# Sparse attention and a multiplicative FFN on one core: strided rows block-major, v cast by its load, probabilities transposed by DMA

## The chip, the cores and the metric

The kernel runs on one core of one Trainium2 chip. The metric is the device time of one execution in microseconds. Three executions of the kernel before took 291.08, 290.63 and 291.65 us; the median is 291.08 us. A separate execution was profiled, and all rows below come from it.

## The reference, cut to what matters

```python
batch, n_heads, seq, head_dim = (8, 8, 576, 64)         # q, k, v in fp32
scores = scale * np.matmul(q, k.transpose(0, 1, 3, 2))
rel = pos[:, None] - pos[None, :]
mask_local = (rel >= 0) & (rel < 32)                    # heads 0 to 3
mask_strided = (rel >= 0) & (pos[None, :] % 32 == pos[:, None] % 32)   # heads 4 to 7
...                                                     # softmax over the masked scores, times v
x = attn_out.transpose(0, 2, 1, 3).reshape(4608, 512)
a = x @ w1                                              # w1, w2: 512 x 1024
b = x @ w2
h = a * b @ w3                                          # w3: 1024 x 1024
out = h @ w_out                                         # w_out: 1024 x 512
```

A strided head attends only among the 18 positions that share a residue modulo 32, so its scores fall into 32 blocks of 18 x 18. A local head attends to a band of 32.

## The kernel before

**Pairs.** The 64 heads are worked in 32 pairs of two heads; pair `i` belongs to batch `i // 4`, and in each batch the first two pairs are local and the last two strided. A pair passes through these steps, each a function of the pair's number:

- `load_qk`: POOL issues loads of q and k that cast fp32 to fp16 on the way, two DMAs for a local pair (line 87), four for a strided one (line 97), into a tile with four buffers.
- `load_v`: SP issues loads of v in fp32, three for a local pair (lines 111, 113), six for a strided pair (line 123). `emit_cast_v` then casts v to fp16 on POOL (line 265 local, line 269 strided), and for a local pair `shift_v` lets SP copy the cast tile to a second one moved by 32 rows (lines 277 and 278, tile `vhL`).
- `emit_T`: TensorE (PE in the profile) transposes q and k (line 289); ACT and DVE copy the results out of PSUM.
- `emit_S`: score matmuls (line 321 local, 328 strided), mask added by DVE. `emit_max`, `emit_sub`, `emit_exp`: maximum and subtraction on DVE, exponential on ACT into `prL` or `prS`.
- `emit_norm`: row sum and reciprocal on DVE (lines 369, 371), product on POOL (line 372). It is called norm(i) below.
- `emit_P`: TensorE transposes the probabilities, five 128x128 blocks for a local pair and six for a strided one (line 382, tile `pp` in PSUM); ACT copies them to SBUF as `pT` (line 385). Called P(i) below.
- `emit_V`: matmuls of v and `pT` (line 402 local, 417 strided), results copied to `xT`, the FFN's input. Called V(i).

Three residues are packed side by side on the partitions in a strided pair: 3 x 18 = 54 rows per head. Row p holds residue group `p // 18` and block `p % 18`.

**FFN.** First w3 and w_out are folded into one 1024 x 512 matrix (`fold_t`, `fold_m`, lines 218 to 229). Then chunks of 512 tokens go through `emit_a` (line 236), `emit_b` (line 246, product on DVE at line 249) and `emit_out` (line 254, copied by ACT, stored by SP at line 258).

**Order.** The order of the work is written out by hand; each engine executes its own instructions in program order. Pairs 0 to 4 are written call by call, then a loop covers n = 5 to 8, then a main loop n = 9 to 33. An iteration n of the main loop issues `load_qk(n+4)`, `load_v(n+3)`, `shift_v(n)`, S(n), V(n-2), T(n+1), max, sub, exp of n, P(n-1), norm(n) and `emit_cast_v(n+1)`. Between them `feed(us, batches)` puts in FFN pieces by a credit of us per call, 5.2 us per iteration in the main loop, as far as the batches needed are there. After the loop, the remaining FFN pieces follow without attention work between them.

**Queues.** SP issues the stores of the output, the loads of v and the shifts; POOL issues the casting loads and also computes. Within each of the two queues the program gives DMAs eight completion semaphores in turn, and a DMA waits for the one eight places before it in its queue to have landed. Whatever stands behind a waiting DMA on POOL waits too, norm among it. The PSUM pool `psA`, with two buffers, holds the transposed q and k and, in turn, `pp`.

Of the kernel before, what the change touches and what calls it, by code (L numbers as in the profile page):

```python
# [8 lines left out]
FP32 = mybir.dt.float32  # L9
# [18 lines left out]
def kernel(  # L28
# [40 lines left out]

    NB = 2  # L70
    staged, cast, qks, prs, pts = {}, {}, {}, {}, {}

    def where(i):
        b, hp = divmod(i, 4)
        return b, hp, hp < 2, (2 * b + hp % 2) % NB

    def load_qk(i):

        b, hp, local, par = where(i)
        h0 = 2 * hp  # L80
        t = ld.tile([P, 2, ST * D], FP16, tag="s16", bufs=4, name="s16")
        if i + 1 == 4 * B:
            for p0 in (0, HALF):
                nc.vector.memset(t[p0 + 32:p0 + HALF, :, (ST - 1) * D:ST * D], 0.0)
        for src, p0 in ((q, 0), (k, HALF)):
            if local:
                nc.gpsimd.dma_start(t[p0:p0 + HALF, :, 0:LB * D],
                                    src[b, h0:h0 + 2].rearrange("h (p j) d -> p h (j d)", j=LB))
            elif i + 1 == 4 * B:
                for r in range(3):  # L90
                    n = ST if r < 2 else ST - 1
                    nc.gpsimd.dma_start(t[p0 + NA * r:p0 + NA * r + NA, :, 0:n * D],
                                        _ap(src[b, h0], 11 * r * D,
                                            [[NR * D, NA], [S * D, 2], [1, n * D]]))
            else:
                for h in range(2):
                    nc.gpsimd.dma_start(t[p0:p0 + SW, h, :],  # L97
                                        _ap(src[b, h0 + h], 0,
                                            [[11 * D, 3], [NR * D, NA], [1, ST * D]]))
        cast[i] = t  # L100

    def load_v(i, gate=False):
# [3 lines left out]
        if local:  # L106
            vt = vsL[par]
            if gate:
                nc.vector.memset(vt[:, 0:LC - 1, 0, 0:1], 0.0)
            for h in range(2):  # L110
                nc.sync.dma_start(vt[:, 0:LC - 1, h, :],
                                  _ap(v[b, h0 + h], 0, [[D, P], [P * D, LC - 1], [1, D]]))
            nc.sync.dma_start(vt[0:HALF, LC - 1],
                              v[b, h0:h0 + 2, P * (LC - 1):S].rearrange("h p d -> p h d"))
        else:
            vt = vsS[par]
            if gate:
                nc.vector.memset(vt[:, :, 0:1], 0.0)
            for r in range(3):
                for half in range(2):  # L120
                    n = 6 if half == 0 else 5 if r < 2 else 4
                    p0 = HALF * half + NA * r
                    nc.sync.dma_start(vt[p0:p0 + NA, :, 0:n * D],
                                      _ap(v[b, h0], (11 * r + 6 * half) * D,
                                          [[NR * D, NA], [S * D, 2], [1, n * D]]))
        staged[i] = vt
# [3 lines left out]
    maskS = consts.tile([P, SW], FP32, name="maskS")  # L130
    sel = consts.tile([3, HALF], FP16, name="sel")
    sel2 = consts.tile([3, 2, HALF], FP16, name="sel2")
# [16 lines left out]
    def make_sel():  # L149
        nc.gpsimd.memset(sel, 1.0)  # L150
        nc.gpsimd.affine_select(out=sel, in_=sel, compare_op=ALU.is_ge, fill=0.0, base=0,
                                pattern=[[1, HALF]], channel_multiplier=-NA)
        nc.gpsimd.affine_select(out=sel, in_=sel, compare_op=ALU.is_ge, fill=0.0, base=NA - 1,
                                pattern=[[-1, HALF]], channel_multiplier=NA)

    def make_maskS():
        for h in range(2):
            nc.vector.tensor_copy(out=sel2[:, h, :], in_=sel)
        mps = psF.tile([P, SW], FP32, tag="f", name="mps")
        nc.tensor.matmul(mps, sel2.rearrange("p h q -> p (h q)"), sel[:, 0:SW], start=True,  # L160
                         stop=True)
# [16 lines left out]
    prS = [wpool.tile([P, 12, HALF], FP16, name=f"prS{i}") for i in range(NB)]  # L178
    vsS = [wpool.tile([P, 2, 6 * D], FP32, name=f"vsS{i}") for i in range(NB)]
    vsL = [wpool.tile([P, LC, 2, D], FP32, name=f"vsL{i}") for i in range(NB)]  # L180
# [80 lines left out]
    def emit_cast_v(i, eng=nc.gpsimd.tensor_copy):  # L261
        b, hp, local, par = where(i)
        vst = staged.pop(i)
        if local:
            eng(out=vhL[par][:, 1], in_=vst)
            pts[i] = [vhL[par]]
        else:
            vh = att.tile(list(vst.shape), FP16, tag="vhS", name="vh")
            eng(out=vh, in_=vst)
            pts[i] = [vh.rearrange("p h (t d) -> p t h d", d=D)]  # L270

# [92 lines left out]
    def emit_norm(i):  # L364
# [8 lines left out]
                                op=ALU.mult)  # L373

    def emit_P(i):

        b, hp, local, par = where(i)
        pr = prs.pop(i)[0]
        n = LC if local else 6
        pp = psA.tile([P, n, P], FP16, tag="tr", name="pp")  # L380
        for s in range(n):
# [6 lines left out]
    def emit_V(i):  # L388
# [20 lines left out]
        else:  # L409
            ops = [psF.tile([P, 6 - half, SW], FP32, tag="f", name="op") for half in range(2)]  # L410
            for s in range(6):
                for half in range(2):
# [3 lines left out]
                    for h in range(2):  # L416
# [4 lines left out]
            nc.scalar.copy(out=_sub(xT[hp], 0, P, x0, [[NR, NA], [11, 3], [1, 6]]),  # L421
                           in_=_sub(ops[0], 0, P, 0, [[1, NA], [NA, 3], [SW, 6]]))
            nc.vector.tensor_copy(out=_sub(xT[hp], 0, P, x0 + 6, [[NR, NA], [11, 2], [1, 5]]),
                                  in_=_sub(ops[1], 0, P, 0, [[1, NA], [NA, 2], [SW, 5]]))
            nc.vector.tensor_copy(out=_sub(xT[hp], 0, P, x0 + 28, [[NR, NA], [1, 4]]),
                                  in_=_sub(ops[1], 0, P, 2 * NA, [[1, NA], [SW, 4]]))

# [3 lines left out]

    NP = 4 * B
    T_A = 0.87
# [31 lines left out]
    with tc.manual_schedule():  # L465
# [54 lines left out]
        emit_cast_v(1)  # L520
        shift_v(1)
        load_qk(5)
        fold_t(3, act)
# [7 lines left out]
        emit_max(3)  # L531
        emit_cast_v(2)
        load_w12(1)
# [8 lines left out]
        emit_norm(3)  # L542
        emit_cast_v(3)
        load_v(4, True)
# [16 lines left out]
        emit_exp(4)  # L561
        load_v(6, True)
        load_v(7)
# [5 lines left out]
        for n in range(5, 9):  # L569
# [8 lines left out]
            if n > 5:  # L578
                emit_V(n - 2)
                load_v(n + 2)  # L580
            emit_sub(n)
# [4 lines left out]
            if n == 8:  # L586
# [3 lines left out]
                shift_v(8)  # L590
                load_v(11)
        for n in range(9, NP + 2):
# [62 lines left out]
```

## Time and profile before

| what | value |
|---|---|
| median of three executions | 291.08 us (290.63 to 291.65) |
| the profiled execution's own time | 291.78 us |
| its span, first to last instruction | 290.1 us |
| mean granted TensorE clock | 0.994 |
| busy: PE, DVE, ACT, POOL | 262.0, 175.8, 157.7, 130.0 us |
| PE transposes of probabilities (line 382), in all 32 pairs | 176 blocks of 128x128 |
| ACT copies of them (line 385) | 32, of 685 ns (local) and 791 ns (strided) |
| POOL casts of strided v (line 269) | 16 of 848 ns |

The table's busy times are unions over the whole span; the parts of the span differ, so they are read together with the windows and chains below. "PE" is the matmul row, "PEld" its weight loads, "SPq" an instruction of SP's queue that only issues. In a chain of waits each line has a start, a length in us and what the time was spent on; in a timeline each line has a start, a length, the engine, the line, the operation, its output and input, and a count, with the idle time before it in brackets.

### The profile page before, as it was taken

What the parts mean: (1) busy time and instruction counts of PE and PEld (TensorE: products, weight loads), DVE (VectorE), ACT (ScalarE), POOL (GpSimd) and SP (SyncE); (2) the same over time, 40 slices, a digit from 0 to 9 for tenths busy, and PEclk for the clock granted to TensorE, in tenths of its full rate; (3) what the DMA queues carried; (4) which work ended last, traced back from release to release, by engine and by line L of the source; (5) the groups of instructions that cost most, each with busy time, mean ns of one, the idle gap of its engine ahead of it and who ended that gap; (6) DMA issues with size and microseconds to landing.
All of it is one profiled execution on the core that took longest, in us unless ns stands there. A gap on an engine that the chain in (4) does not pass through costs nothing.

```text
span 290.1 us, 10150 instructions
## 1 busy us (share of the span) xinstructions
PE 262.0 (90%) x4305; PEld 138.1 (48%) x4305; DVE 175.8 (61%) x342; ACT 157.7 (54%) x282; POOL 130.0 (45%) x186
## 2 busy tenths in 40 slices
PE   1179768987989999999999999999999999999994
PEld 0045434444445555555555555555555554444441
DVE  3716545688658866785788677768857860441210
ACT  3225654544656765676666667756767554333322
POOL 8655737256665644674465456446732210000000
PEclk9999999999979999999999999999999999999999
DMA  7999999946797777765966796778522003000113
GB/s 113 188 211 208 181 214 157 178 94 118 144 190 177 112 157 173 155 101 137 210 102 86 179 190 98 134 170 166 107 96 97 2 2 123 22 2 36 73 52 129
DMA packets 58893, 36.90 MB, mean 127 GB/s; under 512 B 37088, under 2 KB 53216, under 8 KB 58848
## 3 DMA queue, kind: packets, MB, share of 16 engines
q0 software_dynamic: 27584, 14.88, 37.1%
q1 hardware_dynamic: 31264, 21.38, 26.5%
q8 instruction: 33, 0.54, 0.8%
q14 instruction: 12, 0.10, 0.1%
HBM read 39.07 MB, written 9.44 MB: 167 GB/s over the span
## 4 chain that ended last, share of the span: by engine, by line
PE 76%; DMA 8%; POOL 5%; DVE 4%; issue 3%; ACT 2%; SPq 0%; POOLq 0%; DVEq 0%; ACTq 0%
PE ops L254 21%; PE bps L246 20%; PE aps L236 20%; DMA s<-in_k_dram 4%; DMA vhL<-vhL 4%; PE pp L382 3%; PE tpk L289 2%; PE sp L328 2%; PE sp L321 2%; PE op L402 2%; PE op L417 1%; PE tpq L289 1%; PE fps L227 1%; DVE sm L369 1%; DVE tmp L334 1%
## 5 line engine op out<-in xcount | busy, mean ns | idle before, releaser
L249 DVE TENSOR_TENSOR abt<-bps,asb 128x512 f16<-128x512 f32 x72 | 49.6, 688 | 41.0 <-PE bps L246 37.9
L246 PE MATMUL bps<-xT,w2h 128*128 128x512 f16 x288 | 74.1, 380 | 0.0
L236 PE MATMUL aps<-xT,w1h 128*128 128x512 f16 x288 | 74.0, 379 | 0.0
L254 PE MATMUL ops<-wfh,abt 128*128 128x512 f16 x288 | 68.1, 385 | 0.0
L240 ACT COPY asb<-aps 128x512 f32<-128x512 f32 x72 | 42.4, 588 | 35.9 <-PE aps L236 35.8
L257 ACT COPY osb<-ops 128x512 f32<-128x512 f32 x36 | 21.1, 586 | 41.1 <-PE ops L254 37.9
L254 PEld LDWEIGHTS <-abt 128*128 128x128 f16 x288 | 27.4, 99 | 31.5 <-issue 1.7
L372 POOL TENSOR_TENSOR prL<-prL,rc 128x576 f16<-128x576 f16 x16 | 18.3, 1146 | 51.6 <-DVE rc L371 42.6
L246 PEld LDWEIGHTS <-w2h 128*128 128x128 f16 x288 | 26.5, 98 | 30.0
L236 PEld LDWEIGHTS <-w1h 128*128 128x128 f16 x288 | 27.1, 98 | 28.7
L372 POOL TENSOR_TENSOR prS<-prS,rc 128x594 f16<-128x594 f16 x16 | 19.2, 1198 | 41.5 <-DVE rc L371 20.7
L349 DVE TENSOR_TENSOR tmp<-tmp,mx 128x576 f32<-128x576 f32 (+1 forms) x32 | 26.5, 829 | 1.0
L342 DVE TENSOR_REDUCE mx<-tmp 128x9 f32<-128x576 f32 (+1 forms) x32 | 24.1, 753 | 0.2
L385 ACT COPY pT<-pp 128x640 f16<-128x640 f16 (+1 forms) x32 | 23.6, 738 | 0.3 <-PE pp L382 0.3
L334 DVE TENSOR_TENSOR tmp<-sp,maskL 128x320 f32<-128x320 f32 (+1 forms) x32 | 13.2, 453 | 15.9 <-PE sp L321 15.9
L289 PE MATMUL tpq<-id,s 54*64 54x54 f16 (+1 forms) x640 | 17.7, 196 | 5.2 <-DMA s<-in_q_dram 5.1
L97 POOL DMA_DIRECT2D s<-in_k_dram x30 | 18.0, 611 | 6.5 <-DMA w3s<-in_moe_w_dram 2.3
L289 PEld LDWEIGHTS <-s 54*64 54x64 f16 (+1 forms) x1280 | 15.7, 110 | 9.2 <-DMA s<-in_q_dram 6.3
L289 PE MATMUL tpk<-id,s 54*64 54x54 f16 (+1 forms) x640 | 18.4, 198 | 1.8 <-DMA s<-in_k_dram 1.7
L97 POOL DMA_DIRECT2D s<-in_q_dram x30 | 19.1, 643 | 0.4 <-DMA s<-in_q_dram 0.3
L369 DVE TENSOR_REDUCE sm<-prL 128x9 f32<-128x576 f16 x16 | 12.0, 749 | 11.8 <-ACT prL L361 11.8
L361 ACT ACTIVATE prS<-tmp 128x594 f16<-128x594 f32 x16 | 11.2, 699 | 12.1 <-DVE tmp L349 10.2
(75 smaller groups left out, 304.0 us busy)
## 6 DMA issues: line engine op xcount, KB each, us to landing
out_dram<-osb SPq DMA_DIRECT2D x36, 256.0 KB
vsL<-in_v_dram SPq DMA_DIRECT2D x32, 128.0 KB
vsS<-in_v_dram SPq DMA_DIRECT2D x48, 54.0 KB
s<-in_q_dram POOLq DMA_DIRECT2D x16, 144.0 KB, 4.3
s<-in_k_dram POOLq DMA_DIRECT2D x16, 144.0 KB, 5.3
s<-in_q_dram POOLq DMA_DIRECT2D x30, 74.2 KB, 5.7
s<-in_k_dram POOLq DMA_DIRECT2D x30, 74.2 KB, 6.5
w3s<-in_moe_w_dram POOLq DMA_DIRECT2D x4, 512.0 KB, 12.0
```

The lines of the kernel that those rows point to most:

```text
L97: nc.gpsimd.dma_start(t[p0:p0 + SW, h, :], _ap(src[b, h0 + h], 0, [[11 * D, 3], [NR * D, NA], [1, ST * D]]))
L236: nc.tensor.matmul(aps, w1h[:, ci, jc * P:(jc + 1) * P], xT[ci][:, c * NT:(c + 1) * NT], start=(ci == 0), stop=(ci == KC1 - 1))
L240: nc.scalar.copy(out=asb, in_=aps)
L246: nc.tensor.matmul(bps, w2h[:, ci, jc * P:(jc + 1) * P], xT[ci][:, c * NT:(c + 1) * NT], start=(ci == 0), stop=(ci == KC1 - 1))
L249: nc.vector.tensor_mul(abts[c][:, jc, :], bps, abts.pop((c, jc)))
L254: nc.tensor.matmul(ps, abts[c][:, jc, ts * P:(ts + 1) * P], wfh[:, jc, :], start=(jc == 0), stop=(jc == KC2 - 1))
L257: nc.scalar.copy(out=osb, in_=ps)
L289: nc.tensor.transpose(tp[HALF * h:HALF * h + HALF, s, :], s16[p0:p0 + npar, h, s * D:(s + 1) * D], id16[p0:p0 + npar, p0:p0 + npar])
L342: nc.vector.tensor_reduce(out=mx, in_=tmp, axis=AX.X, op=ALU.max)
L349: nc.vector.tensor_tensor(out=tmp, in0=tmp, in1=_sub(mx, 0, P, 0, [[1, nt], [0, w]]), op=ALU.subtract)
L372: nc.gpsimd.tensor_tensor(out=prv, in0=prv, in1=_sub(rc, 0, P, 0, [[1, nt], [0, w]]), op=ALU.mult)
L385: nc.scalar.copy(out=pT, in_=pp)
```

## The change

Three things change.

1. In strided pairs the 54 rows are ordered with the block first: row p now holds block `p // 3` and residue group `p % 3`. The mask's selector, the loads and the copies from PSUM into `xT` follow. For the last pair, whose last row would run past the tensor, the second head is loaded by four smaller DMAs.
2. v of a strided pair is loaded by four DMAs of POOL that cast to fp16 into a tile `vhS` with four buffers, where six fp32 DMAs of SP and a cast on POOL stood. The two cleared fp32 buffers `vsS` go. For the last pair ten DMAs take the place of the four. These loads come later in the written order: `load_v(2)` behind `load_w3(3)`, `load_v(3)` behind `shift_v(1)`, and in the main loop two pairs ahead of use where it was three.
3. From pair 9 on (`XB = 9`) P(i) is a single transposing DMA issued by SP from `prL` or `prS` straight into `pT`, in place of five or six TensorE transposes and one ACT copy. It is issued at the end of iteration i, where P(i) on TensorE stood in the middle of iteration i+1. V(i) stays in iteration i+2.

On POOL a strided pair thus has eight DMA issues where it had four, and no cast. On SP six issues per strided pair go and one transposing DMA per pair comes.

```diff
+    NP, XB = 4 * B, 9
...
+    def strided_rows(i, h, n):
+
+        if i + 1 < 4 * B or h == 0:
+            return [((0, SW), (0, [[NR * D, NA], [11 * D, 3]]), n)]
+        e = NR * D * (NA - 2)
+        return [((0, SW - 6), (0, [[NR * D, NA - 2], [11 * D, 3]]), n),
+                ((SW - 6, SW - 3), (e, [[11 * D, 3]]), n),
+                ((SW - 3, SW - 1), (e + NR * D, [[11 * D, 2]]), n),
+                ((SW - 1, SW), (e + NR * D + 22 * D, [[D, 1]]), n - 1)]
...
                 for h in range(2):
-                    nc.gpsimd.dma_start(t[p0:p0 + SW, h, :],
-                                        _ap(src[b, h0 + h], 0,
-                                            [[11 * D, 3], [NR * D, NA], [1, ST * D]]))
+                    for r0, ap, n in strided_rows(i, h, ST):
+                        nc.gpsimd.dma_start(t[p0 + r0[0]:p0 + r0[1], h, 0:n * D],
+                                            _ap(src[b, h0 + h], 0 + ap[0], ap[1] + [[1, n * D]]))
...
-            vt = vsS[par]
-            if gate:
-                nc.vector.memset(vt[:, :, 0:1], 0.0)
-            for r in range(3):
-                for half in range(2):
-                    n = 6 if half == 0 else 5 if r < 2 else 4
-                    p0 = HALF * half + NA * r
-                    nc.sync.dma_start(vt[p0:p0 + NA, :, 0:n * D],
...
+            vt = att.tile([P, 2, 6 * D], FP16, tag="vhS", bufs=4, name="vhS")
+            if i + 1 == 4 * B:
+                nc.vector.memset(vt[HALF + 32:P, 1, 4 * D:5 * D], 0.0)
+            for half in range(2):
+                for h in range(2):
+                    n = 6 - half
+                    for r0, ap, m in strided_rows(i, h, n):
+                        m = m if half else n
+                        nc.gpsimd.dma_start(vt[HALF * half + r0[0]:HALF * half + r0[1], h, 0:m * D],
+                                            _ap(v[b, h0 + h], 6 * half * D + ap[0],
+                                                ap[1] + [[1, m * D]]))
+            pts[i] = [vt.rearrange("p h (t d) -> p t h d", d=D)]
...
+    def by_dma(i):
+
+        return XB <= i < NP
+
     def emit_P(i):
...
+        if by_dma(i):
+            pT = att.tile([P, n, P], FP16, tag="pTL" if local else "pTS", name="pT")
+            nc.sync.dma_start_transpose(out=pT, in_=pr.rearrange("p t k -> p (t k)"))
+            pts[i].append(pT)
+            return
...
-        for t in vsS:
-            nc.vector.memset(t, 0.0)
-        load_v(2)
-        load_v(3)
         emit_norm(0)
         load_w3(2)
         load_qk(3)
         load_w3(3)
+        load_v(2)
         load_qk(4)
...
         shift_v(1)
+        load_v(3)
         load_qk(5)
...
-            if n + 3 < NP:
-                load_v(n + 3)
+            for i in (n + 3, n + 2):
+                if i < NP and where(i)[2] == (i == n + 3):
+                    load_v(i)
...
-            if n <= NP:
+            if n <= NP and not by_dma(n - 1):
                 emit_P(n - 1)
             feed(0.2 * f, full)
             if n < NP:
                 emit_norm(n)
                 if n + 1 < NP:
                     emit_cast_v(n + 1)
-            feed(0.4 * f, full)
+            feed(0.2 * f, full)
+            if by_dma(n):
+                emit_P(n)
+            feed(0.2 * f, full)
```

More of the change, by code (lines that the diff above doesn't have):

```diff
@@ L130 @@
     maskS = consts.tile([P, SW], FP32, name="maskS")
-    sel = consts.tile([3, HALF], FP16, name="sel")
+    sel = consts.tile([3, 22, 3], FP16, name="sel")
     sel2 = consts.tile([3, 2, HALF], FP16, name="sel2")
@@ L150, in make_sel @@
         nc.gpsimd.memset(sel, 1.0)
[L151 to L154, printed above, removed]
+        for sg in (1, -1):
+            nc.gpsimd.affine_select(out=sel, in_=sel, compare_op=ALU.is_ge, fill=0.0, base=0,
+                                    pattern=[[0, 22], [sg, 3]], channel_multiplier=-sg)
     def make_maskS():
+        sl = sel.rearrange("p a r -> p (a r)")
         for h in range(2):
-            nc.vector.tensor_copy(out=sel2[:, h, :], in_=sel)
+            nc.vector.tensor_copy(out=sel2[:, h, :], in_=sl[:, 0:HALF])
         mps = psF.tile([P, SW], FP32, tag="f", name="mps")
-        nc.tensor.matmul(mps, sel2.rearrange("p h q -> p (h q)"), sel[:, 0:SW], start=True,
+        nc.tensor.matmul(mps, sel2.rearrange("p h q -> p (h q)"), sl[:, 0:SW], start=True,
                          stop=True)
@@ L178 @@
     prS = [wpool.tile([P, 12, HALF], FP16, name=f"prS{i}") for i in range(NB)]
-    vsS = [wpool.tile([P, 2, 6 * D], FP32, name=f"vsS{i}") for i in range(NB)]
     vsL = [wpool.tile([P, LC, 2, D], FP32, name=f"vsL{i}") for i in range(NB)]
@@ L262, in emit_cast_v @@
         b, hp, local, par = where(i)
-        vst = staged.pop(i)
         if local:
+            vst = staged.pop(i)
             eng(out=vhL[par][:, 1], in_=vst)
             pts[i] = [vhL[par]]
[L267 to L270, printed above, removed]
     def shift_v(i):
@@ L579 @@
                 emit_V(n - 2)
-                load_v(n + 2)
+                if n < 8:
+                    load_v(n + 2)
             emit_sub(n)
```

24 lines of the change are left out of this document (7 added, 17 removed).

## The prediction

> **What bounds the kernel now.** I read the page first: busy shares, slices and the chain by engine.
>
> ```profile
> PE 262.0 (90%) x4305; PEld 138.1 (48%) x4305; DVE 175.8 (61%) x342; ACT 157.7 (54%) x282; POOL 130.0 (45%) x186
> ...
> PE   1179768987989999999999999999999999999994
> ...
> DMA  7999999946797777765966796778522003000113
> ...
> PE 76%; DMA 8%; POOL 5%; DVE 4%; issue 3%; ACT 2%; SPq 0%; POOLq 0%; DVEq 0%; ACTq 0%
> ```
>
> PE fills every slice after the first quarter, while the DMA engines are full in the first quarter. So there are two stages with different limits. The windows confirm it; columns are span, then busy us of PE, PEld, DVE, ACT and POOL, clock, DMA share, GB/s.
>
> ```profile
> 0.00:50.00 50.00, 30.17 (x615) 17.92 (x616) 24.75 (x59) 22.19 (x36) 31.51 (x55) 1.00 1.10 183
> 50.00:80.00 30.00, 26.52 (x512) 13.75 (x510) 22.40 (x41) 16.21 (x31) 16.47 (x22) 1.00 0.72 133
> ...
> 131.06:157.82 26.76, 26.76 (x512) 14.45 (x510) 19.94 (x38) 17.59 (x33) 14.44 (x20) 1.00 0.74 143
> ```
>
> The last line is one batch (four iterations) of the main loop: PE is busy for all of it, DVE for 75%, the DMA engines for 74%, POOL for 54%. Every us of PE work taken from there is a us of time, until something else fills 26.76 us. The chain of waits gives the price of P(i) there, a local pair and a strided one:
>
> ```profile
> 92.71 0.28 PE pp L382 x5
> 92.99 0.86 PE aps L236 x4
> ...
> 99.39 0.34 PE pp L382 x6
> 99.73 0.86 PE aps L236 x4
> ```
>
> The transposes hold PE for 0.28 us (five blocks) or 0.34 us (six). The busy union of line 382 is larger (15.1 us for 176 blocks) because it counts pipeline fill that overlaps the next matmul; the step to the next start is what counts.
>
> The timeline of one batch gives the time that a transposing DMA may take. Norm of a local pair ends at 135.35+1.14, its V starts at 142.57:
>
> ```profile
> 135.35 1.14 POOL L372 TENSOR_TENSOR prL<-prL,rc 128x576 f16<-128x576 f16 x1 [3.83 <-DVE rc L371]
> ...
> 142.57 0.20 PE L402 MATMUL op<-pT,vhL 64*64 64x32 f16 x2
> ```
>
> That is 6.1 us; read the same way the next three pairs have 6.2, 6.1 and 6.9.
>
> In the first stage, POOL's queue is on the chain:
>
> ```profile
> 28.67 0.81 POOL L197 DMA_DIRECT2D w1h<-in_moe_w_dram  x1
> 30.85 0.76 POOL L197 DMA_DIRECT2D w2h<-in_moe_w_dram  x1 [1.36 <-DMA s<-in_q_dram]
> ...
> 34.25 0.77 POOL L197 DMA_DIRECT2D w1h<-in_moe_w_dram  x1
> 35.47 0.74 POOL L197 DMA_DIRECT2D w2h<-in_moe_w_dram  x1 [0.45 <-DMA w3s<-in_moe_w_dram]
> 37.51 1.51 POOL L372 TENSOR_TENSOR prS<-prS,rc 128x594 f16<-128x594 f16 x1 [1.30 <-DVE rc L371]
> ```
>
> Each weight load waits in brackets for a DMA eight places earlier, and norm(2) at 37.51 stands behind the last of them.
>
> **The change part by part.**
>
> *P(i) on PE, removed.* Pairs 9 to 31 are 11 local and 12 strided: 11 x 0.28 + 12 x 0.34 = 7.16 us, all on a full PE. Of the 23 ACT copies (685 and 791 ns, 17.0 us) nothing counts: ACT is at 17.6 of 26.8 us per batch, hidden under PE.
>
> *The transposing DMA, added.* The trace has no such operation. It moves 160 KB (local) or 192 KB (strided) inside SBUF. From below: the fastest landing of a q or k load in the loop is 2.8 us from issue, the median 5.4, the slowest 7.1. From the side: the shift of `vhL`, also SBUF to SBUF on SP, 152 KB in two DMAs, takes 5.4 us from the first issue to the last landing at 65.36 (the chain has its last 4.83 us) and 7.1 us at 32.35 in the crowded first stage. I take 5 us, nearest the shift in the loop, with 2.8 and 7.1 as ends. The window of 6.1 us shrinks with the iteration: a batch of 26.76 loses two local and two strided P, 1.24 us, so an iteration goes from 6.69 to 6.38 and the window to 5.8. At 5 us the DMA is hidden, and costs nothing; each us over 5.8 costs about 1 us in each of 23 iterations, because V(i) then holds PE, which executes in order.
>
> On SP the DMA stands behind a store that waits for ACT's copy, at most 1.8 us in the loop's SP waits, while PE is still before that point too; behind it are the next v load and shift, which are needed an iteration or more later. SP loses the twelve strided v issues of each batch, so its queue gets shorter.
>
> ```profile
> 32.93 6.48 DMA vhL<-vhL
> ...
> 65.93 4.83 DMA vhL<-vhL
> ```
>
> The Trainium skill bears on this. Its page "VectorE: DVE Perf Modes", section "The three transpose paths", puts a 128x128 transpose at 1309 ns by DMA and 390 ns on TensorE; this trace has 56 ns of PE's time per block (0.28/5), so only the DMA figure is of use here. As an estimate from that page, six blocks in a row are 7.9 us, and by it the window would not hold. The page "Advanced Engine Details and Errata", section "X-Bar Transpose (TRN2)", instead calls such DMAs as fast as ordinary ones, by which 192 KB would be hidden. The two pages pull apart, and no run here shows either yet.
>
> *POOL in the loop.* Per batch: eight more issues of about 0.62 us (lines 97 and 87 have 0.61 to 0.65), two casts of 0.85 fewer: 14.4 + 5.0 - 1.7 = 17.7 us of 25.5. Hidden: POOL idles 3.8 us ahead of the norm quoted above. The last strided pair issues ten loads each for q/k and for v: 6.2 us before a norm, some 1.6 us late in two iterations; 0, at most 3 us.
>
> *DMA engines in the loop.* 0.74 x 26.76 = 19.8 us of each batch. The v loads read the same bytes. The transposes move 704 KB per batch; at the window's own rate (143 GB/s at share 0.74, so 193) that is 3.7 us: 23.5 of 25.5. Hidden, but with little left.
>
> *The first stage.* Eight v loads of POOL now stand ahead of the second w2h half. It therefore waits for the first w2h half instead of the `w3s` load. That half is issued at 30.85, and the list of DMA issues has 12.9 us to landing: 43.75. Issue 0.75 and norm(2) 1.2 follow, so P(2), at 40.71 before, starts 5.0 us late; this is the upper end, and V(3), behind which all FFN work stands, is late by as much. Lower end: the twelve strided v loads that SP ran among the loads of 13 to 34 us are gone from there. They are 590 KB, at 183 GB/s 3.2 us of full DMA engines; half stood ahead of the k load of pair 2 that the chain waits 12.11 us for, so the stage could gain 1.6 us. I take both together: w2h lands 3.2 us sooner, at 40.55, so norm(2) ends at 42.5 and P(2) is 1.8 us late; PE's idle 3.5 us between 50 and 80 takes some back. +1.5 us, from -1.6 to +5.0. The removed clearing of `vsS` on DVE (1.5 us) lies ahead of norm(0), whose P(0) waits for PE anyway: nothing.
>
> *Row order.* Same bytes, tile sizes and instruction counts; the loads' sources become contiguous in threes. Nothing either way, beyond the ends just given for loads.
>
> **Sum.** 291.78 - 7.16 + 1.5 = 286.1 for the profiled execution, which stands 0.7 us above the median; from the median, 285.4. The case's own range: 291.08 - 7.16 - 1.6 = 282.3 to 291.08 - 7.16 + 5.0 = 288.9.
>
> **The rivals.**
>
> *Slower: V waits for the transpose.* Place: V(i) on PE in iterations 11 to 33. It decides from 6.1 us per DMA, where the iteration is back at 6.69. At the slow end of the rows, 7.1 us, each iteration loses 1.3 us against the hidden case: 285.4 + 23 x 1.3 = 315. At 6.5 us it is 23 x 0.7 more, 301.5. For it: the DMA engines are 74% busy and a shift of similar size took 5.4 us; the transposes are issued just as POOL issues the next loads. Against: at the loop's end DMA is nearly idle, and SP's own queue gets lighter.
>
> *Slower: the transposes take turns.* If they run block after block on one path, 22 blocks per batch must fit into 25.5 us, 1.16 us each. The shift gives 5.4/152x32 = 1.14 us per 32 KB, at the edge, and 1.49 in the first stage, which would make an iteration 8.2 us and the kernel about 326. These are latencies, which overstate what a stream costs per block. By the figure of the page "VectorE: DVE Perf Modes" of the Trainium skill, 1309 ns, a batch would last 28.8 us and the kernel about 285.4 + 23 x 0.82 = 304, an estimate.
>
> *Same: the first stage eats the gain.* The late norm(2) at its 5.0 us, with two more such waits (POOL has 18 DMAs in a row behind norm(3) where it had ten, ahead of norm(4) at 57.34) of 1 us: 291.08 - 7.16 + 7 = 290.9. Against: SP's strided loads are gone from the same stretch.
>
> **How the numbers follow.** Hidden, 285.4: 0.60. V waits: 0.18. Turns: 0.12. First stage eats it: 0.10. The measurement tells no difference under 0.3%, 0.9 us (290.2 to 292.0). Faster: the hidden case whole and 0.03 of V waits with a DMA barely over its window, 0.63. Same: 0.06 of the first stage case. Slower: the remaining 0.31. The range starts at the hidden case's low end, 282.3; it must reach into the slower cases until no more than 0.2 is out, which takes the 6.5 us case and the turns at 304: 282.3 to 304. The likeliest case alone: 282.3 to 288.9.
>
> **What would show it.** Right: no `pp` of pairs 9 and up on the chain; a batch of the loop at about 25.5 us with PE busy throughout; line 402 and 417 waiting for no DMA; in the first 50 us norm(2) near 41. Wrong: PE idle ahead of lines 402 or 417 with `pT` as the releaser, batches over 26.76 us, POOL's norm waiting for loads in the loop, or V(3) later than 49 us (45.9 before).

## The result and the profile after

On the chip of the first measurement the changed kernel took 287.75 (profiled), 287.21, 291.66 and 293.66 us, the kernel before 290.98 us (median of four, 290.63 to 291.65). The ratio is 0.9877 with a 95% interval of 0.9843 to 0.9911, so the change makes the kernel 1.2% faster there; it leaves out the last two executions of the changed kernel, which ran at a mean granted clock of 0.992 and 0.976 where the first two had 0.999. Part of the 1.2% can be the clock: the profiled execution of the kernel before ran at 0.994, and on the chip of the first four experiments the kernel before took 289.1 to 290.3 us in its three executions at 0.997 and above, against a median of 291.8 us over all 19. Later the changed kernel was run again on two chips and came out at 0.9974 (0.9923 to 1.0025) and 0.9967 (0.9918 to 1.0015). So there is a gain, it is small, and in the two later measurements it can't be told from none. What takes it is the subject of the rest.

From the page of the changed kernel, the same rows as were read of the kernel before:

```profile
PE 255.1 (89%) x4178; PEld 131.3 (46%) x4178; DVE 171.2 (60%) x340; ACT 143.1 (50%) x259; POOL 160.4 (56%) x244
...
PE   1188859988979999999989999998999999999994
...
DMA  7999999945769989979995999699766213000113
...
PE 61%; DMA 13%; DVE 9%; POOL 8%; issue 5%; ACT 3%; SPq 0%; POOLq 0%; DVEq 0%; ACTq 0%
```

PE lost 6.9 us of busy time, close to the 7.2 us that were to go. But its row has an 8 in two slices of the loop where there were only nines, the DMA row is now full in most slices of the loop, and DMA has gone from 8% to 13% of the chain. The windows show the same (columns as before: span, PE, PEld, DVE, ACT, POOL, clock, DMA share, GB/s):

```profile
104.20:131.06 26.86, 26.44 (x493) 13.64 (x492) 19.85 (x39) 15.70 (x30) 18.70 (x28) 1.00 1.00 164
131.06:157.82 26.76, 25.74 (x490) 13.33 (x489) 19.43 (x38) 15.03 (x29) 17.42 (x26) 1.00 0.92 155
```

In the last line PE idles for 1.0 us, where it was busy throughout, and the DMA share is 0.92 instead of 0.74; in the line above it is 1.00. The chain of waits says where the idle time comes from. Each line is a start, a length and what it went to; the 24 matmuls of `ops` come once per batch:

```profile
102.13 5.29 PE ops L261 x24
...
114.00 7.00 DMA pT<-prL
...
128.35 5.18 PE ops L261 x24
...
140.49 6.34 DMA pT<-prL
...
155.15 5.18 PE ops L261 x24
...
167.29 6.01 DMA pT<-prL
...
181.52 5.18 PE ops L261 x24
...
208.58 5.18 PE ops L261 x24
```

A batch lasts 26.22, 26.80, 26.37 and 27.06 us by the starts of `ops` (26.75 or so before, 25.5 forecast), and each of the first three has one transposing DMA of a local pair on the chain, 6.0 to 7.0 us long. It is always the second local pair, 13, 17 and 21 here. In the fourth batch V of pair 25 waits 1.28 us; the chain names DVE's mask addition, but by the semaphores in the trace that pair's DMA landed at the same moment (200.38 and 200.40 us), 7.0 us after its issue. SP's queue in the second of these batches, and then PE's timeline at the same place (brackets: idle time before the instruction and what ended it):

```profile
133.78 2.13 SPq L389 DMA_TRANSPOSE pT<-prL  x1
...
136.58 1.13 SPq L116 DMA_DIRECT2D vsL<-in_v_dram  x2
137.76 0.70 SPq L118 DMA_DIRECT2D vsL<-in_v_dram  x1
138.56 0.55 SPq L280 DMA_DIRECT2D vhL<-vhL  x1
139.16 0.59 SPq L281 DMA_DIRECT2D vhL<-vhL  x1
139.85 0.53 SPq L265 DMA_DIRECT2D out_dram<-osb  x1
140.49 2.07 SPq L389 DMA_TRANSPOSE pT<-prL  x1
```

```profile
146.97 0.46 PE L414 MATMUL op<-pT,vhL 64*64 64x32 f16 x34 [1.02 <-DMA pT<-prL]
```

The transposing DMA of the second local pair is issued at 140.49, behind a v load of 160 KB, a shift of 152 KB, stores of 256 KB and the first local pair's own transposing DMA, all issued within 6.7 us. It lands 6.34 us later; V, which would have started 1.02 us earlier, 5.5 us after the issue, waits on PE, and everything behind V waits with it. The first local pair's V at 139.24 stands just as far behind its DMA's issue and waited for nothing: that DMA landed after 5.25 us.

Two readings keep this profile from being taken at face value. First, its span is 4.1 us shorter than that of the kernel before, but 1.7 us of that are the clock's. The window from 82.70 to 85.50, first in the profile of before, then in that of after:

```profile
82.70:85.50 2.80, 2.80 (x8) 0.97 (x8) 1.89 (x3) 0.70 (x2) 1.73 (x3) 0.50 0.97 220
```

```profile
82.70:85.50 2.80, 2.80 (x19) 1.39 (x18) 1.63 (x4) 1.64 (x4) 2.80 (x6) 1.00 0.44 80
```

In the profile of before the granted clock is 0.50 there. The whole stretch at half speed runs from 82.14 to 85.55 us, so it costs 1.7 us. Such a stretch comes in some executions and not in others, of both kernels. Second, the starts of the groups of four `aps` matmuls (the FFN's first product), laid side by side, show the rest: the changed kernel is 1.2 us late at the first, 0.4 us late at 69 us, 1.9 us early at 86 us (the clock's 1.7 are in that step), and from there it gains only another 2.2 us in a loop that has 7.2 us less to do. The waits of the second local pairs 9, 13, 17, 21 and 25, which are 0.40, 0.58, 1.27, 0.84 and 1.45 us by the jumps in that comparison, are 4.5 of the missing 5.0 us.

In the first stage POOL's queue did what was forecast. Its timeline:

```profile
40.47 0.75 POOL L204 DMA_DIRECT2D w2h<-in_moe_w_dram  x1 [3.34 <-DMA w2h<-in_moe_w_dram]
41.23 1.20 POOL L375 TENSOR_TENSOR prS<-prS,rc 128x594 f16<-128x594 f16 x1
```

The second `w2h` half waits for the first, and norm(2) ends at 42.43 us (forecast 42.5).

### The profile page after: what moved, and what is told of

The parts are those of the page before. It is cut to its first block, busy times and chain, and to the rows that moved or that the text cites. A ratio compares the mean times of both kernels' runs of the same rounds, so it can differ in the third digit from the quotient of the medians.

```text
span 286.0 us, 9835 instructions
## 1 busy us (share of the span) xinstructions
PE 255.1 (89%) x4178; PEld 131.3 (46%) x4178; DVE 171.2 (60%) x340; ACT 143.1 (50%) x259; POOL 160.4 (56%) x244
## 3 DMA queue, kind: packets, MB, share of 16 engines
q1 hardware_dynamic: 43936, 20.82, 32.6%
## 4 chain that ended last, share of the span: by engine, by line
PE 61%; DMA 13%; DVE 9%; POOL 8%; issue 5%; ACT 3%; SPq 0%; POOLq 0%; DVEq 0%; ACTq 0%
PE ops L261 20%; PE bps L253 15%; PE aps L243 15%; DMA pT<-prL 8%; DMA vhL<-vhL 4%; POOL vhS L129 3%; PE sp L324 2%; DVE tmp L352 2%; PE fps L234 2%; DVE tmp L337 2%; DVE sm L372 2%; PE tpk L292 2%; PE op L414 2%; PE op L429 1%; PE tpq L292 1%
## 5 line engine op out<-in xcount | busy, mean ns | idle before, releaser
L256 DVE TENSOR_TENSOR abt<-bps,asb 128x512 f16<-128x512 f32 x72 | 49.0, 681 | 43.6 <-PE bps L253 38.6
L261 PE MATMUL ops<-wfh,abt 128*128 128x512 f16 x288 | 65.7, 379 | 0.0
L129 POOL DMA_DIRECT2D vhS<-in_v_dram x70 | 42.0, 678 | 4.8 <-DMA w3s<-in_moe_w_dram 2.6
L243 PEld LDWEIGHTS <-w1h 128*128 128x128 f16 x288 | 27.8, 98 | 32.7
L253 PEld LDWEIGHTS <-w2h 128*128 128x128 f16 x288 | 26.5, 98 | 30.0
L375 POOL TENSOR_TENSOR prL<-prL,rc 128x576 f16<-128x576 f16 x16 | 19.0, 1185 | 14.9 <-DVE rc L374 7.9
L352 DVE TENSOR_TENSOR tmp<-tmp,mx 128x576 f32<-128x576 f32 (+1 forms) x32 | 25.9, 808 | 1.0
L103 POOL DMA_DIRECT2D s<-in_k_dram x35 | 22.3, 717 | 5.4 <-DMA w3s<-in_moe_w_dram 2.3
L103 POOL DMA_DIRECT2D s<-in_q_dram x35 | 21.6, 646 | 0.4 <-DMA s<-in_k_dram 0.4
L234 PE MATMUL fps<-woh,w3T 128*128 128x512 f16 x64 | 16.9, 412 | 1.7 <-ACT w3T L227 1.4
L419 ACT CAST xT<-op 128x320 f16<-128x320 f32 (+1 forms) x32 | 11.2, 403 | 13.9 <-PE op L414 13.9
```

The source lines that it names most:

```text
L103: nc.gpsimd.dma_start(t[p0 + r0[0]:p0 + r0[1], h, 0:n * D], _ap(src[b, h0 + h], 0 + ap[0], ap[1] + [[1, n * D]]))
L129: nc.gpsimd.dma_start(vt[HALF * half + r0[0]:HALF * half + r0[1], h, 0:m * D], _ap(v[b, h0 + h], 6 * half * D + ap[0], ap[1] + [[1, m * D]]))
L234: nc.tensor.matmul(ps, w3T[:, kc, :], woh[:, kc, :], start=(kc == 0), stop=(kc == KC2 - 1))
L243: nc.tensor.matmul(aps, w1h[:, ci, jc * P:(jc + 1) * P], xT[ci][:, c * NT:(c + 1) * NT], start=(ci == 0), stop=(ci == KC1 - 1))
L253: nc.tensor.matmul(bps, w2h[:, ci, jc * P:(jc + 1) * P], xT[ci][:, c * NT:(c + 1) * NT], start=(ci == 0), stop=(ci == KC1 - 1))
L256: nc.vector.tensor_mul(abts[c][:, jc, :], bps, abts.pop((c, jc)))
```

## The experiments

The theory after the first look: the transposing DMA hides in general, but in each batch the second local pair's lands after V's place, because of what stands in front of it at the DMA engines. Two rivals: that the engines simply have too much work in the loop (throughput), so that order does not matter; and that the time came from another part of the change. The first four experiments shared one chip, the next four a second, the last four a third; ratios are to the kernel before on the same chip.

### Parts 1 and 2 alone

```diff
     def by_dma(i):
-        return XB <= i < NP
+        return False
```

> All P(i) back on TensorE and ACT; row order and v loads stay as in the changed kernel. My theory (the transposing DMA's gain of 7.2 us in the loop is given back in waits of V on pT; 1.9 us of the result comes from the first stage and is owed to the new v loads and row order): about 289.1 us, 1.9 under the kernel before, loop batches back at 26.75 us with PE busy throughout. Rival (the other two parts do nothing, the DMA transposes give the whole 3.5 us): within 0.5 us of the kernel before.

Measured: 291.49 us, ratio 0.9992 (0.9955 to 1.0029). Its loop runs exactly as before, 26.75 us per batch with PE full, and the row order and the casting loads of v are worth nothing that can be measured. The 1.9 us that the theory gave to the first stage did not come; 1.7 of them were the clock's. The gain and the loss both belong to part 3. The windows from 105 to 185 us, three batches of the loop, of before and of this kernel:

```profile
105.00:185.00 80.00, 80.00 (x1530) 43.24 (x1529) 59.44 (x115) 53.16 (x97) 43.99 (x60) 1.00 0.73 143
```

```profile
105.00:185.00 80.00, 80.00 (x1530) 43.21 (x1529) 59.49 (x115) 52.67 (x96) 53.38 (x78) 1.00 0.69 132
```

Loading v as fp16 takes 0.04 off the DMA share, and costs POOL 9.4 us of issues in three batches, which are hidden.

### A plain copy in place of the transposing DMA

```diff
-            nc.sync.dma_start_transpose(out=pT, in_=pr.rearrange("p t k -> p (t k)"))
+            nc.sync.dma_start(pT.rearrange("p n k -> p (n k)"),
+                              _sub(pr, 0, P, 0, [[1, n * P]]))
```

> Each transposing DMA is replaced by an ordinary DMA of the same bytes from the same tile to the same tile, so the probabilities stay untransposed. If a transposing DMA costs the DMA engines more than an ordinary one (my theory: it moves packets of 256 bytes, 16256 more of them in the trace, and the engines' share rose from 0.73 to 0.97): landing falls from 5.0 to 5.8 us to about 4, the share to about 0.85, the wait of V goes and the time is 291.0 - 1.9 - 7.2 = 282 us. Rival (it is as fast as an ordinary one and only the crowd of loads makes it late): landing and time stay within 1 us of the changed kernel, 287.5.

This kernel leaves the transposing out, so its output is not the attention's; it only measures time. Measured: 284.80 us, ratio 0.9735 (0.9674 to 0.9796). Nothing waits for `pT` in its profile, and the batches last 25.63, 25.53 and 25.52 us. That is the loop as it was forecast. The same window and the landing times (the last column of the list of DMA issues), first of this kernel, then of the changed one:

```profile
105.00:185.00 80.00, 80.00 (x1483) 41.02 (x1481) 60.05 (x117) 47.10 (x87) 56.56 (x82) 1.00 0.83 168
```

```profile
pT<-prS SPq DMA_DIRECT2D x12, 192.0 KB, 4.0
...
pT<-prL SPq DMA_DIRECT2D x11, 160.0 KB, 4.3
```

```profile
105.00:185.00 80.00, 77.87 (x1469) 40.24 (x1467) 58.89 (x115) 45.36 (x85) 54.14 (x79) 1.00 0.97 160
```

```profile
pT<-prS SPq DMA_TRANSPOSE x12, 5.0
pT<-prL SPq DMA_TRANSPOSE x11, 5.8
```

So the price of transposing can be read in packet time. (The DMA share is the sum of the packets' times over the time of 16 engines. Packets overlap in it, for it came to 1.10 in the first 50 us of the kernel before, so 1.00 is not a limit.) With P on PE the packets take 0.69 x 26.75 = 18.5 us of all 16 engines per batch, with plain copies 0.83 x 25.56 = 21.2, with transposing DMAs 0.97 x 26.5 = 25.7. Four copies cost 2.7 us, four transposing DMAs of the same bytes 7.2, or 1.8 us each: 2.7 times as much. SP's queue over the whole span says nearly the same: its packets take 19.6% of 289.7 us with P on PE, 24.6% of 283.0 with copies and 32.6% of 286.0 with transposing DMAs, which is 0.6 and 1.6 us for each of the 23. By its packet counts (26944, 30256 and 43936) a copy has 144 packets and a transposing DMA 739.

The list's medians are of the landings that it could match, only 6 of 23 in the changed kernel. The semaphores in the traces give all: medians of 2.8 us (strided) and 4.3 us (local) for the copies, 4.4 and 5.2 us for the transposing DMAs. In the four full batches the second local pairs stand apart. Their transposing DMAs take 6.0 to 7.0 us, those of all other pairs 3.6 to 5.9 us, and the second local pairs' copies 4.7 to 5.0 us. That difference is what the window of 5.5 us did not have.

### The second local pair back on TensorE

```diff
     def by_dma(i):
-        return XB <= i < NP
+        return XB <= i < NP and i % 4 != 1
```

> The second local pair of each batch (pairs 9, 13, 17, 21, 25, 29) transposes on TensorE again, all other pairs from 10 on by DMA. My theory (only that pair's DMA lands later than its V, because it is issued into the thickest of the loads): 17 pairs still save 7.16 - 6 x 0.28 = 5.5 us, no wait is left, so 291.0 - 1.9 - 5.5 = 283.6 us, loop batches of 25.8 us. Rival (the DMA engines as a whole are the bound in the loop, busy 92 to 100% there): the wait moves to another pair and the time stays within 1 us of the changed kernel, 287.5.

Measured: 286.51 us, ratio 0.979 (0.9724 to 0.9855); by the ratio that lies between the two expectations. The profiled execution, of 289.89 us, was the longest of the four; in it no wait on a DMA of `pT` is left, the landings are 4.1 and 4.4 us, and the loop gains a steady 0.95 us per batch. Taking six of the 23 pairs back makes the loop better than the whole change did. It does not tell why, since it removes the late DMA and relieves the engines at once.

### V one iteration later

```diff
-        for n in range(9, NP + 2):
-            full = (n - 1) // 4
-            first = full - 1 if n % 4 == 1 else full
+        for n in range(9, NP + 3):
+            late = n > 10
+            full = (n - 1 - late) // 4
+            first = full - 1 if n % 4 == 1 + late else full
...
-            emit_V(n - 2)
+            if n != 11:
+                emit_V(n - 2 - late)
```

> V of every pair from 9 on stands one iteration later (iteration i+3), with nothing else moved. My theory (latency of the DMA, not the DMA engines' throughput, costs the gain): the window grows from 6 to 12 us, no V waits for pT, loop batches of 25.5 us, 291.0 - 1.9 - 7.2 = 282 us. Rival (throughput of the DMA engines): batches stay above 26.3 us because the loads come late instead, and the time stays within 1 us of 287.5.

Measured: 292.27 us, ratio 1.0004 (0.9956 to 1.0052). Both theories missed the time. V waits for `pT` no more, but the tokens of a batch come an iteration later, so the feeds find no FFN piece for a while and the order of the pieces changes. PE then waits for other engines. From its waits, of PE and of PE's weight loads (total us, times, longest):

```profile
PE ops L261 <- DVE abt L256: 1.8, 4, 0.9
PE bps L253 <- DVE abt L256: 1.7, 3, 0.8
PE aps L243 <- DVE xT L437: 1.5, 1, 1.5
```

```profile
PEld L261 <- DVE abt L256: 3.8, 4, 1.4
PEld L243 <- DVE xT L437: 3.3, 5, 2.0
```

This run shows that room for V is not to be had by shifting it alone; on the cause of the late DMA it is inconclusive. Its batches of 26.49 us are what the throughput rival named, but waits for other engines are in them; and the second local pairs' DMAs are still the late ones (6.8 to 8.0 us in the full batches, all others 3.6 to 5.8).

### The local v load behind the transposing DMA

```diff
-            for i in (n + 3, n + 2):
-                if i < NP and where(i)[2] == (i == n + 3):
-                    load_v(i)
+            if n + 2 < NP and not where(n + 2)[2]:
+                load_v(n + 2)
...
             if by_dma(n):
                 emit_P(n)
             feed(0.2 * f, full)
+            if n + 3 < NP and where(n + 3)[2]:
+                load_v(n + 3)
```

A local pair n+3 falls to the iterations of the second local and the first strided pair. On the second chip, and again on the third:

> The load of v of the local pair n+3 is moved behind the transposing DMA of P(n) in SP's queue; nothing else is changed, the bytes stay the same. Theory (order): the second local pair's probabilities land late in each batch because loads issued just ahead of them stand in front of them at the DMA engines. Then this pair's wait at V (0.40, 0.58, 1.27, 0.84 and 1.45 us in the changed kernel, 4.5 us together) goes, the batches come down from 26.2-27.1 to some 25.5-25.8 us, and the time to 283-284.5 us. Rival (throughput): the engines are 0.92 to 1.00 busy in the loop, so whatever order the packets have, some of them are late; then the wait moves to v itself or to the xT loads and the time stays at 287-288.5 us. V of pair n+3 has three iterations, so a landing about 1 us later than now shouldn't be seen by itself.

> The kernel with the load of v of the local pair behind the transposing DMA, repeated beside the changed kernel on the same chip. By the order theory it is 1 to 1.5% below the changed kernel, at 0.975 to 0.983 of before, with no wait on prL's DMA. By the throughput rival the two agree within 0.3% and the earlier difference was the chip's.

Measured: 286.99 us, ratio 0.9813 (0.9718 to 0.9908), and 286.79 us, 0.9804 (0.9724 to 0.9884), beside the changed kernel's 0.9974 and 0.9967 on the same two chips. The same bytes in another order are worth 1.6%. SP's queue in the second run, and PE's V of the same pair:

```profile
163.66 0.54 SPq L280 DMA_DIRECT2D vhL<-vhL  x1
164.25 0.59 SPq L281 DMA_DIRECT2D vhL<-vhL  x1
164.93 0.53 SPq L265 DMA_DIRECT2D out_dram<-osb  x1
167.48 1.22 SPq L389 DMA_TRANSPOSE pT<-prL  x1
168.75 1.64 SPq L116 DMA_DIRECT2D vsL<-in_v_dram  x2
```

```profile
173.07 0.20 PE L414 MATMUL op<-pT,vhL 64*64 64x32 f16 x2
```

V starts 5.6 us after the issue and waits for nothing; in the full batches of this run the second local pairs' DMAs land after 4.5 to 5.4 us. Not every wait is gone: 0.7 us is left at pair 9, whose V stands only 4.6 us behind the issue, and 0.7 us at the strided pair 22 (in the first of the two runs 0.8 us at two strided pairs). The rival is not dead, either: the DMA share is still 0.97 in this loop, the loop's gain is 5.1 of 7.2 us, and the time missed the 283 to 284.5 us that the order alone should have given.

### The strided loads of v earlier

```diff
-            for i in (n + 3, n + 2):
+            for i in (n + 3, n + 4 if n > 9 else n + 2):
```

> From pair 14 on the casting loads of v of the strided pairs are issued four pairs ahead in place of two, that is in the two strided iterations of a batch and not in its two local ones. Theory (order): the local iterations, where the second local pair's probabilities are late, are relieved of two of their loads, so that pair lands at about 5 us in place of 6 and its wait is mostly gone: 284-286 us; the strided iterations get the bytes in their stead and their probabilities land later than 5.0 us, perhaps first at the limit. Rival (throughput): the sum of bytes per batch is the same, the wait only changes its pair: 287-288.5 us.

Measured: 292.24 us (286.65 to 295.47, before 292.49), ratio 0.9874 (0.9793 to 0.9955); with medians that level and a spread that wide, a gain over the changed kernel is not shown. Both expectations were missed. In its profile V of the local pairs still waits 5.6 us in four places, while the strided probabilities land no later than before (median of all twelve 4.5 us against 4.4). By this run POOL's loads are not what the second local pair waits behind; the local v loads, the shift and the store, still ahead of it on SP, may be. Why the waits came out longer than in the first profile stays open.

### Without the local loads of v

```diff
-            for i in (n + 3, n + 2):
-                if i < NP and where(i)[2] == (i == n + 3):
-                    load_v(i)
+            i = n + 2
+            if i < NP and not where(i)[2]:
+                load_v(i)
+            if n + 3 < NP and where(n + 3)[2]:
+                staged[n + 3] = vsL[where(n + 3)[3]]
```

> Leaves out the loads of v of the local pairs from pair 12 on (the cast goes over what lies in the buffer, so their output is not the attention's): 2 x 128 KB less per batch, all else as in the changed kernel. It is a bound on what those loads cost the transposing DMAs. Both theories expect the landing of the local pairs' probabilities to come down from 5.8 to about 4.5-5 us and the wait at V to go: 282.5-284.5 us. If the wait stays although these bytes are gone, neither the order nor the throughput is the cause, and the second local pair is late for a reason at its own issue (SP's queue) or its source (prL).

Measured: 286.38 us, ratio 0.9787 (0.9712 to 0.9862), landings 4.5 and 4.9 us, and of the waits two are left, 1.2 us in all, at pair 9 and at a first local pair, 16. That is above the 282.5 to 284.5 us expected. To leave these loads out is worth no more than to move them behind.

### The changed kernel again, on both chips

> The changed kernel itself, unaltered, on the same chip as the others, so that they can be compared with it directly: 287-288.5 us by both theories, with the wait of the second local pair of each batch as before.

> The changed kernel itself once more, unaltered, with more executions, since it came out 1.2% below the kernel before on one chip and level with it on another. If its gain is the loop's 7.2 us less what the second local pair of each batch loses by its wait at V (4.5 us in one trace, about as much with fewer and longer waits in the other), it lies at 0.985 to 0.998 of before, and its profile again has idle time in front of op (line 414) that ends with the transposing DMA of prL. If the first trace was the typical one, 0.988.

Measured: 292.76 us, ratio 0.9974 (0.9923 to 1.0025), and 291.59 us, 0.9967 (0.9918 to 1.0015). The first missed its 287 to 288.5 us. The second kernel's profile has the longest of these waits; its line of PE's waits, its chain, and PE's timeline at the last one:

```profile
PE op L414 <- DMA pT<-prL: 7.1, 4, 2.8
```

```profile
139.88 7.42 DMA pT<-prL
...
167.69 6.82 DMA pT<-prL
...
195.82 7.22 DMA pT<-prL
```

```profile
203.17 0.46 PE L414 MATMUL op<-pT,vhL 64*64 64x32 f16 x34 [2.81 <-DMA pT<-prL]
```

The late pairs cost 7.1 us here, and 2.3 us as this view counts them in the first profile (3.6 with pair 25, whose wait it puts down to DVE). At the longest, pair 25, the landing is only part: the product on POOL ended at 194.47 us, and SP issued the DMA 1.35 us later, its queue held up by a store that had waited 1.9 us for ACT's copy. By the starts of `aps` the loop loses 1.3 us against before where it should gain 7.2. So the price of the one late pair differs from execution to execution, and it is enough to take the whole gain.

### Both remedies, and the first local pair in the second's place

Local v behind the transposing DMA with `i % 4 != 1` besides; and the order of the changed kernel with `i % 4 != 0`, which takes as many transposing DMAs away per batch, but not the late one:

> Local v behind the transposing DMA, and the second local pair's probabilities back on TensorE and ScalarE. Order theory: the pair taken back was the only late one, and its wait is gone already, so to take it back as well costs 5 x 0.28 us = 1.4 us of TensorE and brings nothing for it: 285.5-287 us on a chip on which before takes 291-292, slower than the load's move alone by up to 0.5%. Rival (throughput): one transposing DMA less per batch relieves the engines and the rest of the small waits on prS and on the abt tiles go too: faster than the load's move alone by 0.3% or more.

> The order of the changed kernel, but the first local pair of each batch (12, 16, 20, 24) has its probabilities on TensorE and ScalarE and the second keeps its DMA: as many transposing DMAs are taken off the engines as when the second was taken back, but behind no loads of v. Order theory: the second local pair's DMA still stands behind the loads, so its wait stays (1 to 2 us in most batches) and the kernel loses 4 x 0.28 us besides: 0.995 to 1.000 of before. Rival (throughput): which pair is taken back does not matter, so the wait goes, as it did then: 0.978 to 0.983.

Measured: 285.26 us, ratio 0.9789 (0.9722 to 0.9856), and 288.03 us, 0.9833 (0.9753 to 0.9912). The first does not differ from the move alone by more than the intervals. The second is what the throughput rival said and the order theory did not: with the first local pair on PE the second one's DMA still stands behind the v loads, and in its profile (of the longest execution, 289.55 us) one wait on `pT` is left, that of pair 9:

```profile
PE op L414 <- DMA pT<-prL: 1.5, 1, 1.5
```

Pair 9's V stands 4.6 us behind the issue, and no first local pair's DMA goes ahead of it in any of these kernels, so its wait is a case of its own: its window is shorter, and why its DMA still takes 6.0 us here is not shown. In the full batches the second local pairs' DMAs land after 4.4 to 5.3 us here.

So neither theory holds alone. What the second local pair's DMA has in front of it is a backlog, made of the first local pair's transposing DMA and the v loads, shift and store behind that. Taking either the first transposing DMA (1.8 us of packet time) or the v load (160 KB) out from in front brings the landing back to about V's 5.5 us. With the order unchanged the second local pairs of the full batches land after 6.0 to 7.0 us in the first profile and 5.6 to 7.4 in the two later ones; with the v load moved or left out after 4.5 to 5.9 (three profiles), with the first pair on PE after 4.4 to 5.3. A loop at a DMA share of 0.97 can work when what is urgent goes first (the move), and one at 0.88 or 0.89 worked in either order.

## Why the prediction was right, and where it was not

*P(i) on PE, removed: right.* The plain copy's batches of 25.5 us are the forecast 25.5; from the ninth group of `aps` to the end of the loop that kernel gains 6.8 of the 7.16 us.

*The transposing DMA at 5 us, hidden: right for most pairs, wrong for one in four.* The medians of all 23 are 4.4 and 5.2 us. The step that failed is "each us over 5.8 costs about 1 us in each of 23 iterations" with one landing time for all of them, together with the sentence that on SP the DMA "stands behind a store". In the second local pair's iteration it stands behind the next v load, a shift, a store and the first pair's transpose, and lands at 6.0 to 7.0 us in the first profile, up to 7.4 in the others. The window was also smaller than the 5.8 us forecast: 5.5 us for most local pairs of the full batches (133.78 to 139.24, above), while the strided ones had 6.0 to 6.9. The rival "V waits for the transpose" was the right mechanism at the right place, with its point near 6 us; it was priced for all 23 iterations, at 301.5 us and more, where it strikes five or six. The forecast and this rival were treated as one or the other, and the kernel does both. The prediction's own signs say so too: of the signs of being right, batches of 25.5 us with PE busy throughout did not come, and of the signs of being wrong two did, PE idle ahead of V with `pT` as the releaser and batches over 26.76 us (26.80 and 27.06).

*DMA engines at 23.5 of 25.5 us per batch: too low.* Their packets take 25.7. The rest of the batch came out lower than counted, 18.5 us for 19.8. The 3.7 us for the transposes were bytes over the window's rate; plain copies take 2.7, transposing ones 7.2. This is the term that was mis-sized, and the one that leaves no room for a backlog.

*Transposes take turns: not at a price that counts.* The last two strided pairs, whose DMAs meet few loads, land 2.5 us after the issue. That is 0.42 us per block for six blocks, latency included, where the rival needed more than 1.16. Whether the blocks run one after another is not shown. The Trainium skill's page "VectorE: DVE Perf Modes", section "The three transpose paths", has 1309 ns for one; this trace shows less per block in a row of them. The Trainium skill's page "Advanced Engine Details and Errata", section "X-Bar Transpose (TRN2)", calls these DMAs as fast as ordinary ones: no run here agrees, medians of 4.4 and 5.2 us stand against 2.8 and 4.3 for the same bytes.

*POOL in the loop: right in its size, not quite in being hidden.* It is busy 17.4 to 18.7 us in three batches and 20.3 in the fourth, against 17.7. But the chain reaches the late DMA of pair 13 through POOL, two v loads (1.19 us from 110.76) and the product behind them (1.16 us from 112.83), and that of pair 9 likewise.

*The first stage: right in its mechanism,* norm(2) at 42.43 us and the first `aps` 1.2 us late against 1.5; by the ninth group it had been given back, and parts 1 and 2 alone came out even.

*The time.* 285.4 was forecast; 287.75 and 287.21 are inside the range, and above by about half the 4.5 us that the late pairs took in that profile. The other half is covered by the first stage, which cost less than the 1.5 us counted, and by luck with the clock: the 291.78 us of the profile before include a half-clock stretch that cost 1.7 us, and the profile after has none. "Faster" was right by the measurement on record; the two later measurements say that it was nearly "same", for the reason given to the slower rival.

## What to carry to other kernels

When work is moved from a full engine to a DMA, ask not for a typical landing time but for that of the worst iteration: list what the issuing queue and the other queues put in front of it within its own window, and put the load that has three iterations' time behind the DMA that has one. Here the change with that reordering, of the same bytes and instructions, stands at 0.980 to 0.981, and without it at 0.988 to 0.997. And count a transposing DMA by the time that its packets take at the engines, not by its bytes.

## What the runs showed of the hardware

- A transposing DMA of 160 to 192 KB from SBUF to SBUF takes 1.6 to 1.8 us of packet time of the 16 DMA engines, a plain copy of the same bytes 0.6 to 0.7 us (worked out above in two ways). It lands after 4.4 us (192 KB) or 5.2 us (160 KB) at the median instead of 2.8 and 4.3. For the last two strided pairs, whose DMAs meet few loads, it is 2.5 us against 2.1 to 2.3.
- Its issue occupies SP's queue for 1.2 us at the median and up to 2.1 us, that of a plain copy for 0.5 us.
- The granted clock falls to 0.50 for 3.4 us now and then (once, in the profile of the second local pair back on TensorE, for 10.2 us), at a cost of about 1.7 us for a stretch of 3.4. In the profile of the kernel before none lies in the gapless main loop. In the traces read here, two of the main loop's sixteen waits of 0.7 us and more at V were followed by one. Seen from the other side, each of the 17 stretches that these traces have before their last matmuls began during a wait of PE of 0.7 us or more or within 2.5 us of its end. In the changed kernel on the second chip one begins 1.1 us behind the wait (windows; the clock is the third number from the right):

```profile
198.00:201.60 3.60, 1.35 (x88) 1.02 (x83) 1.22 (x5) 0.99 (x4) 3.60 (x7) 1.00 1.34 131
201.60:204.60 3.00, 3.00 (x8) 1.06 (x7) 1.74 (x3) 1.31 (x4) 2.24 (x6) 0.50 0.92 125
```

  Here PE had waited 2.25 us, and the stretch added 1.5 us to it. That a wait brings the clock down is suggested by this and not shown: most waits, among them the main loop's longest of 2.81 us, have none behind them.
